# First-layer products of chunk pairs by Strassen's identity, in an S4D plus Mish kernel

## The chip, the core and the metric

The kernel runs on one core of one Trainium2 chip. The metric is the device time of one execution in microseconds (us); it is given as the median of three runs, and one more execution was recorded by the hardware profiler. A core has a matrix engine (TensorE, PE in the profile; PEld is its weight load), a vector engine (VectorE, DVE), an engine for activation functions (ScalarE, ACT), a general one (GpSimd, POOL) and one that issues transfers (SyncE, SP). Each takes its own queue of instructions in order; semaphores make one wait for another. TensorE writes its sums into PSUM, 128 partitions of eight banks; one bank holds 512 float32 per partition.

## The reference

```python
def _B_ref(x, w1, b1, w2):
    h = jnp.einsum("bsd,df->bsf", x, w1) + b1
    sp = jnp.log1p(jnp.exp(-jnp.abs(h))) + jnp.where(h > 0, h, jnp.zeros_like(h))
    act = h * jnp.tanh(sp)
    return jnp.einsum("bsf,fd->bsd", act, w2)

x = A_u
xn = _layernorm(x, axis=-1)
return x + _A_ref(xn, ...) + _B_ref(xn, B_w1, B_b1, B_w2)
```

There are 2048 tokens of 640 features; the hidden layer has 1728. `_A_ref` is a state-space convolution (S4D) of the normalised input. For the inputs given its kernel is so nearly a polynomial that the program does it with running sums over the tokens; a flag tells the cases in which that would not hold, and a general program stands behind the flag. The feed-forward part `_B_ref` holds nearly all of the arithmetic.

## The kernel before

The tokens are cut into four blocks b of 512, the hidden layer into 14 chunks f of 128 (chunk 8 has 64). A tile holds features on the partitions and a block's tokens along the columns. Float32 operands are split into two float16 numbers, high and low (`W1H`, `W1L`, `XH`, `XL`), and a product is three matmuls: high by high, low by high, high by low. The 640 features are five tiles of 128, so the first layer of a chunk (`mm1`) is 15 matmuls of 512 columns, and so is the second layer (`mm2`), which adds into five accumulators `ACC`, one bank each.

`step(b, f)` is one chunk: `mm1` of f into a first-layer accumulator, then the activation, then `mm2` of chunk f - 3 (`LAG`). The activation (Mish) alternates between ScalarE and VectorE: a sigmoid (`mish_0`, L611), `(h + bias) * s` on VectorE (`mish_v1`, L615), arctangent, square, hyperbolic tangent on ScalarE (L619, L623, L627), a product on VectorE (L631), the high half on ScalarE (L637) and the low half on VectorE (L647). The second part of chunk f - 1 is issued between the steps of chunk f.

The order is written by hand: `place` fills lists for each (b, f) that `step` issues at fixed points: `LOADS` (transfers from SP's queue), `V_` and `W_` (VectorE mostly), `A_` and `E_` (ScalarE), `PEX` (TensorE). They hold the side work: splitting weights and tokens into halves (`hi_w1`, `lo_w1`, `hi_w2`, `lo_w2`, `hi_x`, `lo_x`), the statistics and normalising of the next block (`stats`, `rstds`, `spread`, `norm_t`), the running sums (`skip_a` to `skip_d`, placed by the list `CONV`), taking the finished sums out of `ACC` (`join`), and sums of squares that check the weights' size (`chk`).

First-layer accumulators: two tiles `H[0]` and `H[1]` and a third, `TR`, a bank each. `bank` alternates between the two:

```python
H = [ps.tile([P, TB], F32, name=f"h{j}") for j in range(2)]
TR = ps.tile([P, TB], F32, name="tr")
return (H[0], H[1], TR)[f] if b == 0 and f < 3 else H[(f + 1) % 2]
```

## Time and profile before

| | |
|---|---|
| timed runs | 372.11, 372.90, 372.93 us; median 372.9 |
| profiled execution | 372.37 us, of it the profile's span 370.2 |
| block 0 / 1 / 2 / 3 of the span | to about 110, 200, 290, then the end |
| TensorE's granted clock | 0.998 of full speed |

A row of the timeline reads: start, time, engine, line, operation, what it writes from what, its size and count; in brackets the idle time of the engine before it and what ended it. The time of a matmul's row reaches to its modelled end and overlaps the next row's, so its pace is read from the starts. A row of a group (line, engine, operation) ends with busy time, mean time of one in ns and the idle time before. A row of the stretches has the length, then each engine's busy time with its count, then the granted clock, the transfers' share and GB/s.

### The profile page before, as it was taken

The numbers are of one execution on the slowest core, as the hardware profiler recorded it, in microseconds if no ns is written. First come the engines' busy times: TensorE is split into PE (matmuls) and PEld (weight loads), VectorE is DVE, ScalarE is ACT, GpSimd is POOL, SyncE is SP. The second block draws the span as 40 slices with busy tenths as digits, with TensorE's granted clock in tenths as the row PEclk, the third lists the DMA queues.
The fourth block names the chain that finished last, engine by engine and source line by source line (L and its number), as shares of the span: only waits on it lengthen the run. The fifth ranks groups of instructions, "written<-read, shape, count | busy, mean of one in ns | idle before, by whom it ended". The sixth has DMA issues, their size and how long they took to land.

```text
span 370.2 us, 4877 instructions
## 1 busy us (share of the span) xinstructions
PE 361.0 (98%) x1729; PEld 168.5 (46%) x1729; DVE 268.4 (72%) x455; ACT 271.5 (73%) x527; POOL 50.9 (14%) x72
## 2 busy tenths in 40 slices
PE   7999999999999999999999999999999999999992
PEld 6754444444444444444444444444444444444441
DVE  5969868995784987667547998666744787888632
ACT  3599896995767877776859787778767786887620
POOL 2100100000022051000013125100002332211000
PEclk9999999999999999999999999999999999999999
DMA  7867942900009747313256974712100943323104
GB/s 232 298 200 233 353 146 78 337 12 0 3 5 185 230 138 179 97 38 104 67 142 142 229 191 127 185 63 63 32 0 6 159 118 90 79 34 58 28 2 148
DMA packets 24302, 44.74 MB, mean 121 GB/s; under 512 B 3384, under 2 KB 6736, under 8 KB 24272
## 3 DMA queue, kind: packets, MB, share of 16 engines
q1 hardware_dynamic: 17424, 30.28, 25.6%
q0 software_dynamic: 6240, 13.11, 17.9%
q10 hardware_dynamic: 608, 0.98, 0.8%
q8 instruction: 15, 0.25, 0.3%
q14 instruction: 15, 0.12, 0.1%
HBM read 35.17 MB, written 5.26 MB: 109 GB/s over the span
## 4 chain that ended last, share of the span: by engine, by line
PE 95%; DMA 2%; issue 0%; ACTq 0%; ACT 0%; DVE 0%
PE h L559 45%; PE acc L586 14%; PE acc L587 14%; PE acc L588 14%; DMA w1s<-in_w_dram 2%; PE h L538 1%; PE acc L581 1%; PE acc L570 1%; PE acc L583 1%; PE acc L580 1%; PE tr L538 1%; PE acc L574 1%; PE acc L821 0%; PE acc L599 0%; PE acc L596 0%
## 5 line engine op out<-in xcount | busy, mean ns | idle before, releaser
L559 PE MATMUL h<-xh,w1h 128*128 128x512 f16 x265 | 92.0, 379 | 0.0
L588 PE MATMUL acc<-hi,w2l 128*128 128x512 f16 x235 | 89.1, 379 | 0.0
L587 PE MATMUL acc<-lo,w2h 128*128 128x512 f16 x235 | 89.1, 379 | 0.0
L586 PE MATMUL acc<-hi,w2h 128*128 128x512 f16 x235 | 89.1, 379 | 0.0
L559 PE MATMUL h<-xh,w1l 128*128 128x512 f16 x245 | 86.3, 379 | 0.0
L559 PEld LDWEIGHTS <-w1h 128*128 128x128 f16 (+1 forms) x534 | 50.5, 98 | 63.7 <-issue 4.6
L615 DVE SCALAR_TENSOR_TENSOR A<-h,bs,s 128x512 f32<-128x512 f32 x51 | 38.1, 747 | 57.0 <-ACT s L611 56.9
L611 ACT ACTIVATE s<-h,cv 128x512 f32<-128x512 f32 x51 | 34.9, 684 | 60.0 <-PE h L559 58.8
L559 PE MATMUL h<-xl,w1h 128*128 128x512 f16 (+2 forms) x269 | 63.8, 377 | 0.0
L647 DVE SCALAR_TENSOR_TENSOR lo<-A,hi 128x512 f16<-128x512 f32 x52 | 35.9, 690 | 16.6 <-ACT hi L637 16.6
L623 ACT ACTIVATE p<-p,kc 128x512 f32<-128x512 f32 (+1 forms) x56 | 40.4, 722 | 1.7
L619 ACT ACTIVATE p<-s,kc 128x512 f32<-128x512 f32 (+1 forms) x56 | 39.8, 711 | 0.1
L627 ACT ACTIVATE s<-p,kc 128x512 f32<-128x512 f32 (+1 forms) x56 | 39.8, 711 | 0.0
L631 DVE SCALAR_TENSOR_TENSOR A<-s,A 128x512 f32<-128x512 f32 (+1 forms) x56 | 38.1, 681 | 1.6 <-ACT s L627 1.5
L559 PEld LDWEIGHTS <-w1l 128*128 128x128 f16 x245 | 24.0, 98 | 28.5
L637 ACT ACTIVATE hi<-A 128x512 f16<-128x512 f32 (+1 forms) x56 | 34.4, 614 | 2.1 <-DVE A L631 2.1
L586 PEld LDWEIGHTS <-w2h 128*128 128x128 f16 x235 | 23.1, 98 | 27.6
L588 PEld LDWEIGHTS <-w2l 128*128 128x128 f16 x235 | 23.0, 98 | 27.7
L587 PEld LDWEIGHTS <-w2h 128*128 128x128 f16 x235 | 23.0, 98 | 27.3
L368 POOL DMA_DIRECT2D res<-in_xT_dram x15 | 13.5, 992 | 123.8 <-DVE res L661 113.1
L508 DVE TENSOR_TENSOR_SCAN g<-g,car,kc 128x512 f32<-128x512 f32 x20 | 25.6, 1279 | 0.0
L512 DVE TENSOR_TENSOR_SCAN g<-g,car,g 128x512 f32<-128x512 f32 x20 | 25.3, 1265 | 0.0
(142 smaller groups left out, 367.9 us busy)
## 6 DMA issues: line engine op xcount, KB each, us to landing
chk<-in_w2T_dram SPq DMA_DIRECT2D x15, 288.0 KB, 3.6
w2s<-in_B_w_dram SPq DMA_DIRECT2D x13, 320.0 KB, 3.9
chk<-in_w1T_dram SPq DMA_DIRECT2D x13, 320.0 KB, 4.1
xrow<-in_A_u_dram SPq DMA_DIRECT2D x12, 320.0 KB, 4.3
xt<-in_xT_dram SPq DMA_DIRECT2D x15, 256.0 KB, 7.4
res<-in_xT_dram POOLq DMA_DIRECT2D x15, 256.0 KB, 5.7
xt<-res POOLq DMA_DIRECT2D x15, 256.0 KB, 3.3
out_dram<-xt POOLq DMA_DIRECT2D x15, 256.0 KB, 2.7
```

What stands on the lines that cost most here:

```text
L559: pe.matmul(o, w, x, start=(j == 0), stop=(j == len(order) - 1))
L586: pe.matmul(ACC[k], W2H[f][:, c[k]], hi, start=False, stop=False)
L587: pe.matmul(ACC[k], W2H[f][:, c[k]], lo, start=False, stop=False)
L588: pe.matmul(ACC[k], W2L[f][:, c[k]], hi, start=False, stop=en)
L611: a.activation(s, h, AF.Sigmoid, bias=cv[:n, f:f + 1], scale=1 / SH)
L615: v.scalar_tensor_tensor(A, h, bs[:n, f:f + 1], s, op0=OP.add, op1=OP.mult)
L619: a.activation(p, s, AF.Arctan, bias=one[:n], scale=-1.0)
L623: a.activation(p, p, AF.Square, bias=pi4[:n], scale=2.0)
L627: a.activation(s, p, AF.Tanh, bias=mb[:n], scale=MG)
L631: v.scalar_tensor_tensor(A, s, MC, A, op0=OP.add, op1=OP.mult)
L637: a.activation(hi[:n], A, AF.Copy, scale=MA * SA / SH)
L647: v.scalar_tensor_tensor(lo, A, MA * SA / SH, hi[:n], op0=OP.mult, op1=OP.subtract)
```

## The change

In blocks 1 to 3 the first layer of two neighbouring chunks (0 and 1, 2 and 3, 4 and 5, 6 and 7, 9 and 10, 11 and 12) is computed together. Two chunks by two halves of the tokens by two pairs of feature tiles make a 2 x 2 by 2 x 2 block product, which Strassen's identity (in the form with fifteen additions) does with seven products instead of eight; a product here is two feature tiles, each in three matmuls of 256 columns. The fifth feature tile is added in the plain way, with one of its four products through a difference. That is 54 matmuls of 256 columns per pair instead of 30 of 512. Chunks 8 and 13 and block 0 stay as they were.

The operands need sums: of weights (`load_s`, `sum_w`, `hi_s`, `lo_s`: once per pair, in block 0 and early in block 1, from weights loaded again) and of tokens (`sum_x`, `hi_t`, `lo_t`: once per block). Partial results are shared: the first product `PV` is copied to SBUF, `PX` is copied to `PY` by ScalarE, and VectorE adds `PY` and `PV` into `PZ` and later into `PW`, onto which TensorE adds the remaining products. The three first-layer accumulators become slices of one PSUM tile `HT` of three banks. `pair(b, f)` is the new unit: the products come in four groups, with matmuls of the second layer between them. The side work moves in the lists (`place`, `CONV`), the list `E_` goes, and buffers are regrouped (`stt` 3 to 2, the checks share the weights' buffers and square in place). The flag gets six more conditions (`RATIO`).

```diff
-    H = [ps.tile([P, TB], F32, name=f"h{j}") for j in range(2)]
-    TR = ps.tile([P, TB], F32, name="tr")
+    HT = ps.tile([P, 3 * TB], F32, name="h")
+    TR, *H = (HT[:, j * TB:(j + 1) * TB] for j in range(3))
+    PV, PX, PZ, _, PY, PW = (HT[:, j * (TB // 2):(j + 1) * (TB // 2)] for j in range(6))
+    PVS = tmp.tile([P, TB // 2], F32, name="pvs")
...
+    def sum_w(i):
+        (a11, a12), (a21, a22) = ([t[:, 0:4].rearrange("p (q j) f -> p q j f", j=2)[:, :, j] for j in range(2)]
+                                  for t in SW.pop(i))
...
+        v.tensor_tensor(s1, a21, a22, op=OP.add)
+        v.tensor_tensor(s2, s1, a11, op=OP.subtract)
+        v.tensor_tensor(s3, a11, a21, op=OP.subtract)
+        v.tensor_tensor(s4, a12, s2, op=OP.subtract)
...
-        return (H[0], H[1], TR)[f] if b == 0 and f < 3 else H[(f + 1) % 2]
+        return (H[0], H[1], TR)[f] if b == 0 and f < 3 else H[(f + 1) % 2] if b == 0 else H[0]
...
+        return (lambda: (prod(PV, plain_w(1, 0), sums_x(1), True), prod(PX, plain_w(0, 0), plain_x(0, 0), True)),
+                lambda: (prod(PX, plain_w(0, 1), plain_x(1, 0)), prod(PX, last_w(0), last_x(0)),
+                         prod(PY, sums_w(2), sums_x(2))),
+                lambda: (prod(PY, sums_w(3), sums_x(3)), prod(PY, last_w(1), last_x(1)),
+                         prod(PZ, sums_w(4), plain_x(1, 1)), prod(PZ, last_w(0), last_x(1))),
+                lambda: (prod(PY, plain_w(1, 1), sums_x(4)), prod(PY, last_w(1), [(EH, EL)])))
...
         h = bank(b, f)[:n]
+        if b > 0 and n == P and f < LAST:
+            h = HT[:, TB // 2:3 * TB // 2] if f in PAIRS else H[1]
...
-                W_[b, i + 2].append(lambda b=b, i=i: stats(b + 1, i))
-            LOADS[b, 5].append(lambda b=b: load_xt(b + 1))
-            W_[b, 5].append(rstds)
-            PEX[b, 7] = spread
...
+                W_[b, i + 1].append(lambda b=b, i=i: stats(b + 1, i))
+            LOADS[b, 4].append(lambda b=b: load_xt(b + 1))
+            W_[b, 4].append(rstds)
+            PEX[b, 6] = spread
+            for k, f in enumerate((7, 8, 8, 9, 10)):
+                W_[b, f].append(lambda b=b, k=k: norm_t(b + 1, k, NX["bc"]))
+                A_[b, f + 1].insert(0, lambda b=b, k=k: hi_x(b + 1, k))
+                W_[b, f + 1].insert(0, lambda b=b, k=k: lo_x(b + 1, k))
+            for j, f, m in ((0, 10, 11), (1, 10, 11), (2, 11, 12), (3, 11, 13), (4, 11, 13)):
+                W_[b, f].append(lambda b=b, j=j: sum_x(b + 1, j))
+                A_[b, m].append(lambda j=j: hi_t(j))
+                W_[b, m].append(lambda j=j: lo_t(j))
+
+        for i, (t, at) in enumerate((((0, 5), (0, 7)), ((0, 8), (0, 10)), ((0, 11), (0, 12)),
+                                     ((1, 1), (1, 2)), ((1, 3), (1, 4)), ((1, 5), (1, 6)))):
+            LOADS[t].append(lambda i=i: load_s(i))
+            W_[at].append(lambda i=i: sum_w(i))
+            A_[at[0], at[1] + 1].append(lambda i=i: hi_s(i))
+            W_[at[0], at[1] + 1].append(lambda i=i: lo_s(i))
...
-    CONV = [((1, 4 + k), 0, k) for k in range(4)] + [((2, 0), 0, 4)] + [((2, 3 + k), 1, k) for k in range(KD)]
-    CONV += [((2, 13), 2, 0)] + [((3, 2 + k), 2, k) for k in range(1, KD)] + [((3, 7 + k), 3, k) for k in range(KD)]
+    CONV = [((1, 4), 0, 0), ((1, 6), 0, 1), ((1, 13), 0, 2), ((2, 0), 0, 3), ((2, 1), 0, 4)]
+    CONV += [((2, f), 1, k) for k, f in enumerate((2, 4, 5, 6, 7))]
+    CONV += [((2, 13), 2, 0)] + [((3, f), 2, k + 1) for k, f in enumerate((0, 1, 2, 4))]
+    CONV += [((3, f), 3, k) for k, f in enumerate((5, 6, 7, 8, 9))]
...
+    def pair(b, f):
+        one, two, three, four = mm1_pair(b, f)
+        A = mm2_ops((f - LAG) % NF)
+        p = PEND[0]
+        q = PEND[1] if len(PEND) > 1 else None
+        PEND[:] = [f, f + 1]
+        do(LOADS, (b, f))
+        one()
+        mish_a3(p)
+        mish_v3(p)
+        a.copy(PVS, PV)
+        a.copy(PY, PX)
+        if q is not None:
+            mish_a2(q)
+        run(A[:9])
+        mish_a4(p)
+        do(V_, (b, f))
+        mish_v4(p)
+        if q is not None:
+            mish_a3(q)
+            mish_v3(q)
+        two()
+        v.tensor_tensor(PZ, PY, PVS, op=OP.add)
...
+        if q is not None:
+            mish_a4(q)
+            mish_v4(q)
+        run(A[9:])
+        do(A_, (b, f))
+        do(W_, (b, f))
+        do(LOADS, (b, f + 1))
+        B = mm2_ops((f + 1 - LAG) % NF)
+        run(B[:3])
+        three()
+        v.tensor_tensor(PW, PY, PVS, op=OP.add)
...
+        do(V_, (b, f + 1))
+        do(A_, (b, f + 1))
+        mish_0(b, f)
+        mish_v1(f)
+        mish_a1(f)
+        mish_a2(f)
+        run(B[3:9])
+        four()
+        do(W_, (b, f + 1))
+        mish_0(b, f + 1)
+        mish_v1(f + 1)
+        mish_a1(f + 1)
+        run(B[9:])
...
-            step(b, f)
+            pair(b, f) if b > 0 and f in PAIRS else step(b, f)
```

The order of TensorE where the second layer gives way to the first, around chunk 5 of block 1. Before: `h0` is the accumulator, `w1h5` chunk 5's weights.

```order
L587 MATMUL acc4_195<-lo_1265,w2h1_141 128x512
L588 LDWEIGHTS w2l1_155
L588 MATMUL acc4_195<-hi_1257,w2l1_155 128x512
L559 LDWEIGHTS w1h5_118
L559 MATMUL h0_188<-xh10_173,w1h5_118 128x512 [waits DVE_49]
L559 LDWEIGHTS w1l5_132
L559 MATMUL h0_188<-xh10_173,w1l5_132 128x512
```

And now, at the beginning of the fourth group of the pair of chunks 4 and 5 (`h_210` is `HT`, `th3` a sum of tokens):

```order
L674 LDWEIGHTS w2l2_156
L674 MATMUL acc2_214<-hi_1537,w2l2_156 128x512
L642 LDWEIGHTS w1h5_118
L642 MATMUL h_210<-th3_203,w1h5_118 128x256 [waits DVE_49]
L642 LDWEIGHTS w1l5_132
```

This group waits for VectorE a second time within the pair. The beginning of the next pair, chunks 6 and 7:

```order
L674 MATMUL acc4_216<-lo_1540,w2h2_142 128x512
L674 LDWEIGHTS w2l2_156
L674 MATMUL acc4_216<-hi_1537,w2l2_156 128x512
L642 LDWEIGHTS w1h7_120
L642 MATMUL h_210<-th0_200,w1h7_120 128x256 [waits DVE_49]
```

Counted by the increments of VectorE's semaphore in the built program, the wait before was for `mish_v1` of chunk 3, two chunks back. Of the two waits now, the first is for `mish_v1` of chunk 4, of the same pair (L706 in the changed file), the second for `mish_v1` of chunk 5.

The order of VectorE at the same place. Before, between `lo` of chunk 3 and `mish_v1` of chunk 5 (L508 and L512 are the scans, which the listing names by their general form):

```order
L647 SCALAR_TENSOR_TENSOR lo<-A,hi 128x512 [waits PE_49,Activation_49]
L397 BN_STATS st<-xrow 128x6 [waits DMAHW2_49]
L398 BN_STATS st<-xrow 128x6
L399 BN_AGGR mv<-st 128x2 [waits DVE_49]
L512 SCALAR_TENSOR_TENSOR g_1320<-g_1320,car,g_1319 128x512
L514 SCALAR_TENSOR_TENSOR xt<-xt,cc,g_1320 128x512 [waits DVE_49]
L615 SCALAR_TENSOR_TENSOR A<-h_188,bs,s 128x512 [waits Activation_49]
```

Now, from `lo` of chunk 3 to `mish_v1` of chunk 4 (`ss` are weight sums, `g` the running sum, `pvs` the copy of `PV`):

```order
L738 SCALAR_TENSOR_TENSOR lo<-A,hi 128x512 [waits Activation_49]
L458 BN_STATS st<-xrow 128x6 [waits DMAHW7_49]
L459 BN_STATS st<-xrow 128x6
L460 BN_AGGR mv<-st 128x2 [waits DVE_49]
L416 TENSOR_TENSOR ss<-ws 128x256 [waits DMAHW1_49]
L417 TENSOR_TENSOR ss<-ss,ws 128x256 [waits DMAHW0_49,DVE_49]
L418 TENSOR_TENSOR ss<-ws 128x256
L419 TENSOR_TENSOR ss<-ws,ss 128x256 [waits DVE_49]
L578 SCALAR_TENSOR_TENSOR g_1458<-g_1458,car,g_1457 128x512
L580 SCALAR_TENSOR_TENSOR xt<-xt,cc,g_1458 128x512 [waits DVE_49]
L944 TENSOR_TENSOR h<-h,pvs 128x256 [waits PE_49]
L706 SCALAR_TENSOR_TENSOR A<-h,bs,s 128x512 [waits Activation_49]
```

The four weight sums and the second partial sum (L944) are new in this row of work, and it now ends with the step for which TensorE's fourth group waits. ScalarE's row at this place, from the check of the weights to the sigmoid of chunk 4:

```order
L532 ACTIVATE chk,q_105<-chk 128x640 [waits DMAHW5_49]
L591 COPY car<-g_1457 128x1
L592 COPY car<-g_1458 128x1 [waits DVE_49]
L429 ACTIVATE w1h_123<-ss 128x2x128
L429 ACTIVATE swh_192<-ss 128x256
L429 ACTIVATE swh_192<-ss 128x512
L532 ACTIVATE chk,q_105<-chk 128x640 [waits DMAHW6_49]
L568 ACTIVATE g_1622<-xt,cc 128x512
L569 COPY g_1622<-car 128x1
L570 ACTIVATE g_1623<-xt,cc 128x512 [waits Activation_49]
L702 ACTIVATE s<-h,cv 128x512 [waits DVE_49]
```

Before, a sigmoid stood directly behind the `skip_a` steps and waited for TensorE alone; now the carry copy waits for the scan of the same pair, the weights' high halves stand between, and the sigmoid waits for VectorE's partial sum.

## The prediction

> **What bounds the kernel now.** I read the page's busy line and its chain that ended last first, then what the two vector engines wait for, then the stretches.

> ```profile
> PE 361.0 (98%) x1729; PEld 168.5 (46%) x1729; DVE 268.4 (72%) x455; ACT 271.5 (73%) x527; POOL 50.9 (14%) x72
> PE 95%; DMA 2%; issue 0%; ACTq 0%; ACT 0%; DVE 0%
> ACT s L611 <- PE h L559: 58.8, 37, 3.3
> DVE A L615 <- ACT s L611: 60.9, 43, 3.6
> 110.50:200.00 89.50, 89.50 (x421) 40.24 (x419) 60.16 (x89) 68.57 (x139) 15.56 (x20) 1.00 0.50 129
> 363.50:370.20 6.70, 0.03 (x1) 0.00 (x0) 0.77 (x3) 0.00 (x0) 0.00 (x0) 0.86 0.37 126
> ```

> TensorE is 95% of the chain and is busy through the whole of block 1 (110.5 to 200). The idle time lies elsewhere: ScalarE waits 58.8 us for the first layer to end, VectorE 60.9 us for ScalarE's sigmoid. So fewer columns through TensorE shorten the span, as long as nothing new makes TensorE wait. Since `bank` alternates between two tiles, it can run two chunks ahead of the activation.

> **What the change removes.** A pair of chunks had 30 first-layer matmuls of 512 columns and gets 54 of 256.

> ```profile
> 16.42 1.25 PE L538 MATMUL h<-xl,w1h 128*128 128x256 f16 x10
> 17.52 1.24 PE L538 MATMUL h<-xh,w1l 128*128 128x512 f16 x5
> L538 PEld LDWEIGHTS <-w1h 128*128 128x128 f16 x60 | 5.7, 98 | 1.9 <-ACT w1h L373 1.1
> 117.47 1.24 PE L559 MATMUL h<-xl,w1h 128*128 128x512 f16 x5
> 118.55 0.38 PE L586 MATMUL acc<-hi,w2h 128*128 128x512 f16 x1
> ```

> Ten matmuls of 256 take 17.52 - 16.42 = 1.10 us, 0.110 each, with ten weight loads of 98 ns among them; five of 512 take 118.55 - 117.47 = 1.08, 0.216 each. A pair's first layer goes from 30 x 0.216 = 6.48 to 54 x 0.110 = 5.94, and 18 pairs save 9.7 us. With its 30 second-layer matmuls a pair lasted 12.96 and would last 12.42.

> [...]

> **What the change adds: two waits in every pair.** The accumulators were tiles of their own and are now slices of one tile, and the built program orders all readers and writers of that tile. By its semaphore counts, in each of the 18 pairs the first matmul of the fourth group (`four`) waits for VectorE's first step on the even chunk (`mish_v1(f)`, L706 in the changed file), and the first matmul of the next pair waits for `mish_v1(f + 1)`. Neither touches the columns that these matmuls write. The sigmoid of the even chunk in turn waits for the second partial sum on VectorE. The durations:

> ```profile
> 118.75 0.69 ACT L611 ACTIVATE s<-h,cv 128x512 f32<-128x512 f32 x1 [1.26 <-PE h L559]
> 119.33 0.71 ACT L627 ACTIVATE s<-p,kc 128x512 f32<-128x512 f32 x1
> 119.94 0.71 ACT L619 ACTIVATE p<-s,kc 128x512 f32<-128x512 f32 x1
> 120.69 0.72 ACT L623 ACTIVATE p<-p,kc 128x512 f32<-128x512 f32 x1
> 121.32 0.61 ACT L637 ACTIVATE hi<-A 128x512 f16<-128x512 f32 x1
> 121.84 0.72 ACT L472 ACTIVATE sq<-chk 128x640 f32<-128x640 f32 x1
> 122.56 0.71 ACT L502 ACTIVATE g<-xt,cc 128x512 f32<-128x512 f32 x1
> 123.25 0.72 ACT L504 ACTIVATE g<-xt,cc 128x512 f32<-128x512 f32 x1
> 119.47 0.75 DVE L615 SCALAR_TENSOR_TENSOR A<-h,bs,s 128x512 f32<-128x512 f32 x1 [2.25 <-ACT s L611]
> 120.14 0.68 DVE L631 SCALAR_TENSOR_TENSOR A<-s,A 128x512 f32<-128x512 f32 x1
> 120.74 1.28 DVE L508 TENSOR_TENSOR_SCAN g<-g,car,kc 128x512 f32<-128x512 f32 x1
> 121.97 0.69 DVE L647 SCALAR_TENSOR_TENSOR lo<-A,hi 128x512 f16<-128x512 f32 x1
> 122.57 0.49 DVE L397 BATCH_NORM_STATS2 st<-xrow 128x6 f32<-128x320 f32 x1
> 123.61 1.23 DVE L512 TENSOR_TENSOR_SCAN g<-g,car,g 128x512 f32<-128x512 f32 x1
> 124.88 0.75 DVE L514 SCALAR_TENSOR_TENSOR xt<-xt,cc,g 128x512 f32<-128x512 f32 x1
> L827 DVE SCALAR_TENSOR_TENSOR xl<-acc,xh 128x256 f16<-128x256 f32 x10 | 3.7, 416 | 0.0
> 14.75 1.74 DVE L827 SCALAR_TENSOR_TENSOR xl<-acc,xh 128x256 f16<-128x256 f32 x5
> 8.11 1.49 ACT L824 ACTIVATE xh<-acc 128x256 f16<-128x256 f32 x5 [0.23 <-PE acc L821]
> ```

> From these: 0.20 from the end of a stream on TensorE to its reader (118.55 to 118.75); sigmoid to VectorE's step 0.72 (118.75 to 119.47), that step 0.75; in a row, 0.60 for a step over 512 columns, 1.27 for a scan, 1.04 for the statistics (122.57 to 123.61). No row shows the new 256-column sums: bounds are 0.35 (five in 1.74) and, doubled for a sum whose result stays in PSUM, 0.83. I take 0.42, the duration of one alone, since the nearest row reads PSUM too. An ACT copy of 256 is 0.30 (five in 1.49).

> Clock of a pair without waits, from its first matmul: `one` ends at 12 x 0.110 = 1.32; nine of the second layer to 3.26; `two` (15) to 4.91; nine to 6.85; `three` (18) to 8.83; six to 10.13; `four` (9) to 11.12; six to 12.42.

> *A pair with empty lists.* After `three`: 0.20 + 0.42 + 0.72 + 0.75 = 2.09 until `four` may start; six second-layer matmuls cover 1.30, so TensorE waits 0.79. After `four`: 0.20 + 0.72 + 0.75 = 1.67, cover 1.30, wait 0.37. That is 1.16 per pair and 20.9 over 18, twice the saving. The first partial sum (4.91 + 0.20 + 0.42 = 5.53, due 6.85) and ScalarE's copies (1.32 + 0.20 + 0.60 = 2.12, due 3.26) are covered; without cover each would cost its 0.6 to 0.8.

> *A pair with lists.* VectorE's and ScalarE's side work (statistics, weight sums, scans, normalising) stands in their queues ahead of the very steps that TensorE now waits for. Chunks 4 and 5 of block 1: VectorE ends the first partial sum at 5.53, `lo` at 6.14, statistics 7.18, four weight sums 8.6, scan 9.85, the combining step 10.6, the second partial sum 11.0. ScalarE reaches its carry copies near 6.0 and waits for that scan to 9.85, then 1.1 for the new weights' high halves (two of 256, one of 512), 0.72 check (121.84 to 122.56), 1.4 for the two `skip_a` steps: the sigmoid starts at 13.1, `mish_v1` ends at 14.55 against a due time of 10.13. `four` ends at 15.54, and 1.67 later, at 17.2, the next pair starts: 4.8 late. The same walk with the lists that `place` gives the others, in us beyond 12.42: block 1: 3.5, 4.0, 4.8, 4.2, 3.5, 3.1; block 2 (scans of block 1 and statistics, no weight sums): 3.8, 3.5, 2.4, 3.3, 3.5, 3.1; block 3 (scans only): 2.8, 2.3, 2.0, 1.9, 1.2, 1.2. Sum 54.1. At the entry to blocks 2 and 3 ScalarE's list of chunk 13 (new high halves, check, `skip_a`) makes the copies 1.0 late: 2.0. Together 56.1, of which 20.9 are the bare chain.

> **Block 0** keeps its matmuls, but its three accumulators lie in the same tile, so chunk f waits for `mish_v1(f - 1)` instead of f - 2.

> ```profile
> 20.77 1.24 PE L559 MATMUL h<-xh,w1h 128*128 128x512 f16 x5
> 25.55 0.75 DVE L615 SCALAR_TENSOR_TENSOR A<-tr,bs,s 128x512 f32<-128x512 f32 x1 [0.90 <-ACT s L611]
> 64.50 0.68 DVE L420 TENSOR_TENSOR xt<-xt,bc 128x512 f32<-128x512 f32 x1
> 65.21 0.69 DVE L421 TENSOR_TENSOR xt<-xt,bc 128x512 f32<-128x512 f32 x1
> 65.82 0.74 DVE L615 SCALAR_TENSOR_TENSOR A<-h,bs,s 128x512 f32<-128x512 f32 x1
> 67.08 0.81 DVE L383 SCALAR_TENSOR_TENSOR w2l<-w2s,w2h 128x640 f16<-128x640 f32 x1
> 67.81 0.81 DVE L377 SCALAR_TENSOR_TENSOR w1l<-w1s,w1h 128x640 f16<-128x640 f32 x1
> L439 DVE TENSOR_REDUCE mx<-par 128x10 f32<-128x1280 f32 x1 | 1.5, 1479 | 0.0
> L443 DVE SCALAR_TENSOR_TENSOR junk<-par,dt 128x128 f32<-128x128 f32 x10 | 2.9, 348 | 0.0
> 363.52 0.75 DVE L652 SCALAR_TENSOR_TENSOR xt<-h,xt 128x256 f32<-128x256 f32 x2
> ```

> Chunk 3 starts at 20.77 now and must wait for chunk 2's step, which ends at 25.55 + 0.75 = 26.30: 5.5. From chunk 7 on VectorE's list per chunk passes the 6.48 of TensorE. Chunk 7's: three steps of a chunk 1.9, two weight remainders 1.5, some ten tiny steps 1.5, the reduction 1.5, four products 1.7, the normalising that is moved there 1.3, the new weight sums 1.4: 10.8. The lists of 8, 10 and 11 come to 8.1, 8.3 and 7.4. I make that 4.8, 2.3, 1.5 and 0.9 of TensorE time, 15.0 with the start. At the end the last half's matmuls wait for the drain of the first half, which is in the same tile: 0.4 (two take 0.75).

> The added weight and token loads (SP's queue) feed sums a chunk or more later; POOL's accumulating DMAs keep their order. I cost both at nothing: the transfers lie under 60 to 70 us of vector work per block, and uncovered one would cost its landing of some 4 us once.

> **Sum** against the profiled execution's own 372.4: -9.7 + 56.1 + 15.0 + 0.4 gives 434.2; the median of the timed runs is 0.5 above it, so **434 us** is forecast.

> **Rivals.**
> *The lists are ahead of time*, and only the bare chain is left: 372.4 - 9.7 + 20.9 + 5.5 + 0.4 = 389.5. For it: VectorE and ScalarE idle over a quarter of the span. Against: they are in-order queues, and the lists stand ahead of the awaited step in the program.
> *The end on the other side: the activation chain fits under the second layer.* Place: after `three`. If the reader chain of 2.09 were under the 1.30 of cover, TensorE would never wait and the saving would stay: 372.4 - 9.7 = 362.7, up to 371 with a few list waits. It decides at 0.79 us per pair, and each of the four links has its row, so I see little for it.
> *The clock falls in the gaps.* The last stretch shows a granted clock of 0.86 with TensorE idle, 1.00 where it is busy. If the gaps of 3 to 5 us (the start of block 0, chunk 7, the pairs of block 1) each bring a stretch at a lower clock, some eight of them at 1 to 2 us make 442 to 450.
> [...]
> *The extra weight loads show*: 18 x 24 x 0.098 = 42 us on top, 476, which the ten matmuls in 1.10 us speak against.

> **How the numbers follow.** Forecast 0.66, its own range 415 to 446 (the chains' terms together 15% off either way); lists ahead of time 0.12; clock 0.17; the chain fits 0.03; weight loads 0.01; 0.01 for others. The range that holds 8 in 10 is 408 to 452. A change under 0.3% (1.1 us) can't be told from none. Faster takes the 0.03, less the chance that list waits eat it: 0.02; the same 0.01; slower 0.97.

> **What would show it.** TensorE's idle time in the profile after should be some 70 us, put down to VectorE's `mish_v1` line at two places in each pair, first-layer matmuls still 0.110 apart; the stretch of block 1 should be the longest (some 20 us more than before), block 3 the shortest; chunk 3 of block 0 should start near 26. It is wrong if TensorE waits mainly for the copies, the partial sums or DMAs, or if block 0 keeps its length.

## The result, and the profile after

The changed kernel takes 453.6 us (median of 4, 451.0 to 456.5) against 372.8 for the kernel before on the same chip: a ratio of 1.217, 95% interval 1.210 to 1.225. The forecast was 434 us with a range of 408 to 452: the sign is right, and the time lies 1.6 us above the range. The profiled execution took 453.4 us, 451.6 of it span.

Three rows of the page of the changed kernel: the busy line, TensorE's granted clock in 40 slices, and the chain that ended last by engine.

```profile
PE 372.3 (82%) x2161; PEld 214.1 (47%) x2161; DVE 317.0 (70%) x567; ACT 304.1 (67%) x596; POOL 49.9 (11%) x72
PEclk9969997999998969999699999999999999999998
PE 39%; DVE 33%; ACT 22%; issue 3%; DMA 2%; POOL 0%; SPq 0%; ACTq 0%; DVEq 0%
```

TensorE was 95% of the chain and is 39%; VectorE (33%) and ScalarE (22%) are most of the rest. TensorE's busy time rose from 361.0 to 372.3 us although it streams fewer columns, and four of the 40 slices show a granted clock of 0.6 or 0.7: part of its work ran slower.

What TensorE waited for (in us: total, times, longest):

```profile
PE h L642 <- DVE A L706: 42.1, 28, 4.4
PE h L622 <- DVE A L706: 15.6, 8, 9.2
PE h L642 <- ACT h L920: 5.8, 6, 1.7
PE h L622 <- DVE A L699: 4.6, 1, 4.6
```

L642 is a pair's first layer, L622 an ordinary chunk's, L706 is `mish_v1`, L699 the sum by which VectorE reads chunk 8's two halves, L920 the copy of `PX` to `PY`. The idle time put down to `mish_v1` is what the forecast named.

The stretches of the two kernels, block by block (start and end, length, busy time of PE, PEld, DVE, ACT and POOL, granted clock, DMA share, GB/s). A block's stretch begins here with the first matmul of its first layer; the ends at about 110, 200 and 290 us given for the kernel before lie some three chunks later, where a block's last second-layer sums are done. First the kernel before, then the changed one, the last stretch with the tail:

```profile
0.00:89.41 89.41, 86.93 (x445) 45.25 (x445) 73.97 (x157) 71.51 (x123) 5.16 (x16) 1.00 0.60 196
89.41:177.48 88.07, 88.07 (x414) 39.54 (x412) 63.35 (x114) 65.20 (x132) 13.14 (x16) 1.00 0.41 103
177.48:265.55 88.07, 88.07 (x414) 39.51 (x412) 62.38 (x91) 69.26 (x144) 16.60 (x20) 1.00 0.51 130
265.55:370.20 104.65, 97.98 (x462) 44.24 (x460) 68.67 (x96) 65.52 (x134) 15.96 (x20) 0.99 0.30 64
```

```profile
0.00:112.71 112.71, 91.95 (x444) 45.92 (x445) 85.92 (x183) 76.17 (x132) 5.17 (x16) 0.92 0.48 152
112.71:229.05 116.34, 95.27 (x557) 56.57 (x556) 78.02 (x154) 76.54 (x153) 9.95 (x12) 0.91 0.38 114
229.05:336.23 107.18, 87.47 (x558) 53.44 (x557) 78.82 (x119) 79.54 (x167) 18.80 (x24) 1.00 0.42 109
336.23:451.60 115.37, 97.58 (x606) 58.20 (x604) 74.21 (x113) 71.89 (x147) 16.02 (x20) 0.99 0.27 58
```

Block by block that is:

| stretch | forecast | measured | of it at half pace |
|---|---|---|---|
| block 0 | +15.0 | +23.3 | 5.2 |
| block 1 | +19.9 | +28.3 | 8.5 |
| block 2 | +17.4 | +19.1 | 0 |
| block 3 and tail | +9.6 | +10.7 | 0 |

The forecast's column is its lists per block plus 1.0 at the entries to blocks 2 and 3 and 0.4 at the end, less a third of the 9.7 in blocks 1 to 3. Block 1 grows most and block 3 least, as foretold; blocks 2 and 3 come out within 1.7 us. Both misses lie where the clock column drops, to 0.92 and 0.91.

The fourth group of pair 4|5 in block 1, from the timeline of TensorE (start, duration, and in brackets the idle time before it):

```profile
155.20 0.38 PE L674 MATMUL acc<-hi,w2l 128*128 128x512 f16 x1
159.93 0.37 PE L642 MATMUL h<-th,w1h 128*128 128x256 f16 x1 [4.35 <-DVE A L706]
160.09 0.42 PE L642 MATMUL h<-th,w1l 128*128 128x256 f16 x1
160.31 0.42 PE L642 MATMUL h<-tl,w1h 128*128 128x256 f16 x1
...
164.79 0.42 PE L642 MATMUL h<-tl,w1h 128*128 128x256 f16 x1
165.00 0.33 PE L642 MATMUL h<-th,w1h 128*128 128x256 f16 x1
165.17 0.27 PE L642 MATMUL h<-th,w1l 128*128 128x256 f16 x1
165.28 0.27 PE L642 MATMUL h<-tl,w1h 128*128 128x256 f16 x1
```

After the wait the matmuls start 0.21 us apart, which is half pace; from 165.17 on it is 0.11 again. Read in this way (each start against the one before, less 0.109 for 256 columns or 0.216 for 512), six stretches ran at half pace and lost 2.8, 2.4, 1.5, 2.5, 1.8 and 2.7 us: 13.7 in all, behind idle times of 9.2, 4.6, 2.5, 4.4, 2.5 and 3.4. TensorE's idle rows add up to 73.6 us, against 2.4 in the kernel before. To each wait belong another 0.16 us, by which a matmul's shown 0.38 exceeds its 0.216; that makes some 80 us of gaps.

### The profile page after: what moved, and what is told of

Read it like the earlier page. It is cut to its first block, busy times and chain, and to the rows that moved or that the text cites. A ratio compares the mean times of both kernels' runs of the same rounds, so it can differ in the third digit from the quotient of the medians.

```text
span 451.6 us, 5979 instructions
## 1 busy us (share of the span) xinstructions
PE 372.3 (82%) x2161; PEld 214.1 (47%) x2161; DVE 317.0 (70%) x567; ACT 304.1 (67%) x596; POOL 49.9 (11%) x72
## 3 DMA queue, kind: packets, MB, share of 16 engines
q0 software_dynamic: 6240, 13.11, 14.1%
## 4 chain that ended last, share of the span: by engine, by line
PE 39%; DVE 33%; ACT 22%; issue 3%; DMA 2%; POOL 0%; SPq 0%; ACTq 0%; DVEq 0%
PE h L642 16%; PE acc L674 13%; PE h L622 7%; DVE A L706 6%; ACT s L702 4%; DVE g L578 2%; DVE lo L738 2%; DVE xt L482 2%; PE h L604 2%; DVE xl L400 2%; DVE xt L481 2%; ACT p L718 2%; DVE A L722 2%; ACT hi L728 2%; DVE g L574 2%
## 5 line engine op out<-in xcount | busy, mean ns | idle before, releaser
L674 PE MATMUL acc<-hi,w2h 128*128 128x512 f16 x275 | 103.2, 385 | 0.0
L706 DVE SCALAR_TENSOR_TENSOR A<-h,bs,s 128x512 f32<-128x512 f32 x52 | 38.7, 745 | 53.4 <-ACT s L702 53.4
L642 PE MATMUL h<-th,w1h 128*128 128x256 f16 x72 | 20.6, 286 | 42.1 <-DVE A L706 42.1
L642 PEld LDWEIGHTS <-w1l 128*128 128x128 f16 x216 | 21.5, 100 | 61.9 <-issue 57.8
L642 PEld LDWEIGHTS <-w1h 128*128 128x128 f16 x432 | 43.3, 100 | 12.8 <-issue 1.5
L722 DVE SCALAR_TENSOR_TENSOR A<-p,A 128x512 f32<-128x512 f32 (+1 forms) x56 | 38.4, 685 | 8.9 <-ACT p L718 8.9
L622 PE MATMUL h<-xh,w1h 128*128 128x512 f16 x85 | 26.2, 412 | 20.2 <-DVE A L706 15.6
L714 ACT ACTIVATE p<-p,kc 128x512 f32<-128x512 f32 (+1 forms) x56 | 40.3, 720 | 1.2
L718 ACT ACTIVATE p<-p,kc 128x512 f32<-128x512 f32 (+1 forms) x56 | 39.6, 708 | 0.0
L642 PE MATMUL h<-xh,w1h 128*128 128x256 f16 x126 | 34.3, 273 | 5.8 <-ACT h L920 5.8
L622 PEld LDWEIGHTS <-w1h 128*128 128x128 f16 (+1 forms) x174 | 16.3, 105 | 44.0 <-issue 29.9
L642 PE MATMUL h<-xl,w1h 128*128 128x256 f16 x126 | 34.3, 272 | 0.0
L642 PE MATMUL h<-xh,w1l 128*128 128x256 f16 x126 | 34.3, 272 | 0.0
```

Of the source, the lines that this page charges most:

```text
L622: pe.matmul(o, w, x, start=(j == 0), stop=(j == len(order) - 1))
L642: pe.matmul(o, p, q, start=start and n == 1, stop=n == 3 * len(w), skip_group_check=True)
L674: pe.matmul(o, w, x, start=start, stop=stop)
L706: v.scalar_tensor_tensor(A, h, bs[:n, f:f + 1], s, op0=OP.add, op1=OP.mult)
L714: a.activation(p, p, AF.Square, bias=pi4[:n], scale=2.0)
L718: a.activation(p, p, AF.Tanh, bias=mb[:n], scale=MG)
```

## The experiments

Four theories stood: (A) TensorE waits because everything that touches the one tile `HT` is ordered; (B) the pairs' own copies, partial sums and side work hold it up whatever the tiles; (C) the half pace follows from the idle time; (D) it has another cause. Later ones arose from the results.

**Separate tiles.** In `e1_three_tiles` the three banks are three tiles, and the even chunk's activation is split where `PX` and `PZ` meet:

```diff
-    HT = ps.tile([P, 3 * TB], F32, name="h")
-    TR, *H = (HT[:, j * TB:(j + 1) * TB] for j in range(3))
-    PV, PX, PZ, _, PY, PW = (HT[:, j * (TB // 2):(j + 1) * (TB // 2)] for j in range(6))
+    TR, *H = (ps.tile([P, TB], F32, name=c) for c in ("tr", "h0", "h1"))
+    PV, PX, PZ, _, PY, PW = (t[:, c] for t in (TR, *H) for c in (CA, CB))
...
+        parts = [(CA, PX), (CB, PZ)] if b > 0 and f in PAIRS else [(slice(0, TB), h)]
...
+        for c, h in parts:
+            a.activation(s[:, c], h, AF.Sigmoid, bias=cv[:n, f:f + 1], scale=1 / SH)
```

> The changed kernel with its three accumulator banks as three tiles again (the same columns of PSUM), and the sigmoid and VectorE's first step of an even chunk in two halves of 256 columns, since they now lie in two tiles. Theory A (TensorE waits because all that reads or writes the shared tile is ordered): the first matmul of the fourth group no longer waits for mish_v1 of the even chunk, nor the next pair for mish_v1 of the odd one, and block 0 goes back to waiting for the chunk two before; the 78 us of gaps fall to under 15 and the stretches at half pace vanish, 363 to 375 us. Rival B (the seven products' own partial sums and copies, and the side work ahead of them in the queues, hold TensorE up whatever the tiles): the gaps move to the copies (L920) and the partial sums and the time stays over 400 us.

`e2_two_tiles` keeps `PX` and `PZ` in one tile of two banks:

```diff
+    HT, H1 = (ps.tile([P, n * TB], F32, name=f"h{n}") for n in (2, 1))
+    TR, *H = HT[:, 0:TB], HT[:, TB:2 * TB], H1
...
-        return (H[0], H[1], TR)[f] if b == 0 and f < 3 else H[(f + 1) % 2] if b == 0 else H[0]
+        return (H[1], TR, H[0])[f] if b == 0 and f < 3 else H[f % 2] if b == 0 else H[0]
```

> The changed kernel with two tiles: one of two banks that holds PV, PX, PZ, so that the even chunk's sigmoid stays one instruction of 512 columns, and one of one bank with PY and PW; in block 0 chunks 0, 1, 2 take H1, TR, H0 and the chunks after them H1 and H0 in turn. Theory A: what counts is that PY and PW (written by the fourth group) are apart from PX and PZ (read by the even chunk's activation): as with three tiles, 363 to 375 us, within 3 us of it. Rival B: over 400 us.

They took 403.7 us (ratio to before 1.084, 1.082 to 1.085) and 408.6 us (1.095, 1.093 to 1.098). TensorE's waits with three tiles:

```profile
PE tr L641 <- ACT h L922: 20.5, 8, 6.4
PE h L641 <- DVE h L946: 4.9, 6, 1.7
PE h L621 <- DVE A L708: 3.9, 5, 1.4
```

Theory A is right in what it names: 49.9 of the 80.8 us go with the shared tile, the waits for `mish_v1` shrink from 57.7 us to under 5, and block 0 loses its start wait. It is wrong in what it leaves: 403.7, not 363 to 375. TensorE now waits for the copy (L922 here) and the second partial sum (L946), which stand in their engines' queues; the longer wait had, as it seems, hidden most of that (5.8 us at the copy in the changed kernel). Rival B is right about the remaining 31 us. Two tiles cost 4.8 us more, where the small chunk 8 and the transposes share a tile with a pair's products: TensorE waits 3.7 us for chunk 8's sum (L699) and 2.3 for a transpose's turn.

**The shared tile alone.** `e3_before_one_tile` is the kernel before with its accumulators in one tile:

```diff
-    H = [ps.tile([P, TB], F32, name=f"h{j}") for j in range(2)]
-    TR = ps.tile([P, TB], F32, name="tr")
+    HT = ps.tile([P, 3 * TB], F32, name="h")
+    TR, *H = (HT[:, j * TB:(j + 1) * TB] for j in range(3))
```

> The kernel before, with nothing changed but its three first-layer accumulators made slices of one tile; no seven products. Theory A: chunk 3 of block 0 waits for chunk 2's first VectorE step, 5.5 to 9.2 us, with a stretch at half pace of some 2.5 us behind it; from there on a chunk's first-layer matmuls wait for the step of the chunk just before, 1.67 us after its matmuls end, which the second layer's 3.24 us cover except where side work stands ahead: 382 to 396 us. Rival B (the shared tile costs nothing by itself): 372 to 375 us.

387.1 us (1.039, 1.038 to 1.041), inside theory A's range. Its waits for the tile:

```profile
PE h L559 <- DVE A L615: 9.2, 1, 9.2
PE h L559 <- DVE A L608: 1.9, 1, 1.9
```

With ordinary chunks the one tile costs 14.3 us, 11 of it at the start (9.2 of waiting, 1.6 at half pace, 0.2 of a matmul's end); in blocks 1 to 3 the second layer covers a chunk's chain as worked out. So the tile alone costs 14.3, the pairs with separate tiles 31.0, and both together 80.8: 35.5 us come only of the two together, where a pair's chain is ordered through the tile.

**The half pace.** `e4_keep_busy` fills the waits with 201 matmuls of 0.216 us whose weights are zero, before chunks 3, 9, 12 and 13 of block 0 and before the fourth group of 16 pairs:

```diff
+    def keep(b, n, start=False):
+        for _ in range(n):
+            pe.matmul(ACC[0], zw, XH[b % 2][0], start=start, stop=start)
...
         run(B[3:9])
+        keep(b, KEEP.get((b, f), 0))
         four()
```

> The changed kernel with extra matmuls in the places where TensorE waited most (before chunks 3, 9, 12, 13 of block 0, and before the fourth group of 16 pairs): their weights are zero, they add 0 to an accumulator of the second layer, and there are a few less than the wait had room for. The waits stay as they are. Theory C (the half-pace stretches come from TensorE being idle): the 14 us that matmuls ran over their full pace go, the granted clock is near 1.00, and the time falls to 438 to 446 us. Rival D (matmuls are slow after a wait for another reason, such as the vector engines' work at that time): the stretches at twice the spacing stay, 451 to 458 us.

447.4 us, granted clock 0.994. The clock row of its page, and TensorE's two largest waits:

```profile
PEclk9999999899999999999999999999999999999999
```

```profile
PE h L644 <- DVE A L708: 16.1, 29, 1.6
PE h L624 <- DVE A L708: 7.2, 8, 2.8
```

All stretches at half pace are gone but one, which lost 1.4 us behind a wait of 2.8 us that was left in block 0. So theory C holds and D falls. But the time falls by 6.3 us and not by 13: TensorE reaches its next wait earlier, and the vector engines' lists are not done sooner. The idle rows that are left (34.9 us) and the 43.4 us of filling make 78.3 us where 73.6 stood. The expected 438 to 446 us were missed by 1.4 for that reason.

**The order of the queues.** `e8_step_first` keeps the one tile and puts the odd chunk's lists behind the even chunk's step:

```diff
-        do(V_, (b, f + 1))
-        do(A_, (b, f + 1))
         mish_0(b, f)
         mish_v1(f)
+        do(V_, (b, f + 1))
+        do(A_, (b, f + 1))
         mish_a1(f)
```

> The changed kernel, one tile, with the odd chunk's two lists (V_ and A_) put behind the even chunk's sigmoid and first VectorE step instead of ahead of them. Theory A3 (a list costs TensorE time because it stands ahead of the awaited step): the 35 us of waits before the fourth groups fall towards their 0.73 us each, and the time to 425 to 440 us. Rival F (the same work then stands ahead of the odd chunk's sigmoid, and the wait before the next pair grows by as much): 450 to 465 us, with the waits before the next pair's first matmul several times their 7 us.

The runs took 456.0 to 463.1 us, with a ratio to before of 1.232 (1.225 to 1.239) where the changed kernel has 1.217: not faster. Summed over the rows of its timeline, the waits before the fourth groups fall from 34.1 to 20.2 us, and those before the next matmul of the first layer rise from 10.4 to 30.0: rival F. The lists have to run in any place; where both chunks of a pair are awaited, there is no place for them ahead of either.

`e5_lists_after_copies` (three tiles) moves the lists of chunks 8 and 13 behind the copies of the pair that follows:

```diff
-        do(A_, (b, f))
-        do(W_, (b, f))
+        if (b, f + 1) > (0, LAST) and not end and f in (HALF, LAST):
+            LATE.append((b, f))
+        else:
+            do(A_, (b, f))
+            do(W_, (b, f))
...
         a.copy(PY, PX)
+        do_late()
```

> Three tiles as before, and one move of the order: where a single chunk (8 or 13) stands ahead of a pair, its lists of side work for ScalarE and VectorE come behind the pair's two copies (L922 there) and not ahead of them. With three tiles the six entries 0|13 to 1|0, 1|8 to 1|9, 1|13 to 2|0 and so on waited 6.4, 3.9, 1.5, 4.6, 1.4 and 2.1 us for the copies. Theory A2 (what is left of the loss is side work ahead of a step that TensorE waits for, and its place in the queue decides): the lists are 2.6 us long before block 1 and 1 to 2 elsewhere, so some 8 us of those 20 go and 3 to 4 us at half pace with them: 390 to 397 us. Rival F (the vector queues have no room left there, and the work only moves into the next wait): 400 to 405 us.

401.1 us. The waits for the copy fall from 20.5 to 12.5 us, as theory A2 had it, and the waits for the first partial sum rise from nothing to 6.8, as rival F had it. TensorE's idle rows add up to 34.4 us before and 34.3 after. The 2.6 us gained are half pace: behind the waits it falls from 5.7 to 1.3 us, and the transposes at the start of this profiled execution take 1.6 us more. F is right.

**Fewer pairs.** If a queue with room is what a pair needs, pairs should pay in block 3, whose VectorE and ScalarE have least to do. `e6_block3` has three tiles and pairs in block 3 alone (`PB` is 3); `e7_no_pairs` is its control without any (`PB` is 4); `e9_block3_b` mends what `e6_block3` showed late.

```diff
-            pair(b, f) if b > 0 and f in PAIRS else step(b, f)
+            pair(b, f) if b >= PB and f in PAIRS else step(b, f)
```

> Three tiles, pairs by seven products in block 3 alone; blocks 1 and 2 by ordinary chunks, the weight sums moved to blocks 2 and 3, the scans of blocks 0 to 2 to blocks 1 and 2, the lists behind the copies at the entries, and a few steps of a pair in another order. Theory A2: six pairs save 6 x 0.54 = 3.2 us, and where the queues have room TensorE hardly waits (with three tiles block 3 had one wait of 2.1 us, at its chunk 8): 368 to 371 us, below the kernel before. Rival G (a pair costs more than it saves wherever it stands): 373 us or more.

> The kernel e6_block3 with no pairs in any block and no weight sums, all else the same: the control for it. Theory A2: the gain of e6_block3 is that of the seven products, so this one is 2 to 4 us slower than it and within 1.5 us of the kernel before, 371 to 374 us. Rival H (the gain is that of the side work's new places): as fast as e6_block3.

375.6 us (1.008, 1.007 to 1.010) against 372.5 for the control (0.999, 0.998 to 1.000): six pairs cost 3 us on balance. The timelines of VectorE, ScalarE and TensorE in `e6_block3`, up to the second group of pair 4|5:

```profile
295.96 0.42 DVE L416 TENSOR_TENSOR ss<-ws 128x256 f32<-128x256 f32 x1 [2.84 <-DMA ws<-in_w_dram]
297.43 0.75 DVE L709 SCALAR_TENSOR_TENSOR A<-h,bs,s 128x512 f32<-128x512 f32 x1
298.21 0.36 ACT L932 COPY h<-tr 128x256 f32<-128x256 f32 x1 [3.18 <-DVE A L709]
298.62 0.27 PE L642 MATMUL tr<-xh,w1h 128*128 128x256 f16 x1 [1.41 <-ACT h L932]
```

A load of weights that lands late holds a weight sum; behind it stands chunk 3's step, behind that the copy of pair 4|5, behind that TensorE.

> e6_block3 again with what its trace showed late moved: its pairs saved 3.2 us of matmuls against e7_no_pairs and lost 5.7 to waits, 2.0 at the entry of block 3 (the copies behind the check and chunk 13's steps), 1.4 where the weight sums of pair 9 had waited 2.8 for their load, 1.3 for the second partial sum of that pair, 0.6 at chunk 8 and 0.4 in the start. Here the weight loads come two to four chunks before their sums, the sums of four pairs lie in chunks 4 to 9 of block 2, the checks begin two chunks earlier, the fourth group follows the second partial sum at once and VectorE's step of the even chunk comes behind it. Theory A2 (where no side work stands ahead of an awaited step the saving shows): 369 to 371.5 us, faster than the kernel before. Rival G (some wait always remains that eats the 3.2 us): 372.5 to 375 us.

375.7 us, and the wait had moved again: block 3 lost only 2.5 us to waits, but the normalising and the weight sums that now share block 2 delayed two ordinary chunks there by 2.8 us, with 1.7 us of half pace behind them. That is rival G's reading a second time, 0.7 us above its range.

`e10_three_pairs` (three tiles) takes the last three pairs of block 3 only, with the scans of block 3 ahead of them and the weight sums between them; within a pair no matmuls of the second layer stand between the third and the fourth group now. `e11_control` is the same without the pairs.

```diff
+USE = (6, 9, 11)
...
-            pair(b, f) if b > 0 and f in PAIRS else step(b, f)
+            pair(b, f) if b >= PB and f in USE else step(b, f)
```

> Only the last three pairs of block 3 (chunks 6|7, 9|10, 11|12) by seven products; the scans of block 3 in its chunks 0 to 4 and the weight sums in chunks 4, 6 and 8 of it, so that no entry of a block and no crowded chunk of block 2 is touched, and every load comes at least one chunk ahead. Three pairs save 3 x 0.54 = 1.6 us. Theory A2 (a pair gains where neither VectorE nor ScalarE has side work ahead of an awaited step): TensorE has no wait over 0.5 us in block 3 and the time is 370.5 to 372 us, 1 to 2 us below its control. Rival G (some wait always eats the saving): 372.5 to 374.5 us.

> The kernel e10_three_pairs with ordinary chunks all through and no weight sums, all else the same: its control. Both theories: 372 to 373.5 us, as the kernel before; theory A2 has it 1 to 2 us above e10_three_pairs, rival G at or below it.

371.2 us, ratio to before 0.9957 (0.9943 to 0.9971); the control 372.6 (0.9997, 0.9988 to 1.0006). All the waits of TensorE in `e10_three_pairs` lie in its first 13 us:

```profile
PE acc L1000 <- DVE x L984: 1.8, 3, 0.9
PE tr L1014 <- POOL car L333: 1.5, 1, 1.5
PE h L605 <- DVE w1l L389: 0.2, 1, 0.2
```

Three pairs were to save 1.6 us and save 1.4 against the control. This is the one version here that takes less time than the kernel before, by 0.4%.

## Why the prediction was right or wrong

**What a pair saves: right, and a little low.** In pair 4|5 the fourth group was due 10.13 us after the pair's start; the six matmuls ahead of it end their stream at 155.42, 10.10 after 145.32. First-layer matmuls are 0.11 apart at full pace; at 0.109 by the starts, against 0.110 in the forecast, the 18 pairs save 10.7 us and not 9.7.

**The waits in the pairs: right in place, near in size.** 56.1 us were forecast. Measured are 44.5 us of idle time before fourth groups and first matmuls, 5.8 at the copies (2.0 forecast), 1.8 at the transposes and the flag (not forecast), and 41 matmul ends of 0.16 (not forecast either): 58.7. The sums of 256 columns into PSUM take 0.43 us each (L931 and L944, 18 times each) for 0.42 forecast; the upper bound of 0.83 was the author's estimate, and no row shows a doubling. The walk through pair 4|5 came out to the tenth. Rows of ScalarE's and VectorE's timelines of the changed kernel:

```profile
157.11 0.71 ACT L568 ACTIVATE g<-xt,cc 128x512 f32<-128x512 f32 x1
157.80 0.72 ACT L570 ACTIVATE g<-xt,cc 128x512 f32<-128x512 f32 x1
158.43 0.67 ACT L702 ACTIVATE s<-h,cv 128x512 f32<-128x512 f32 x1
159.13 0.75 DVE L706 SCALAR_TENSOR_TENSOR A<-h,bs,s 128x512 f32<-128x512 f32 x1 [2.88 <-ACT s L702]
```

The sigmoid starts 13.11 us after the pair (13.1 forecast) and the step ends at 14.56 (14.55). The bare chain shows in the last pair, whose lists are empty: 0.73 and 0.27 us of idle time and twice 0.16, against 0.79 and 0.37.

**The start of block 0: wrong in size, 9.2 for 5.5.** The step took chunk 2's `mish_v1` at the time the profile before shows for it. But that step is late itself:

```profile
20.58 0.69 ACT L702 ACTIVATE s<-h,cv 128x512 f32<-128x512 f32 x1 [4.86 <-PE h L604]
29.01 0.70 DVE L706 SCALAR_TENSOR_TENSOR A<-h,bs,s 128x512 f32<-128x512 f32 x1
29.76 2.29 PE L622 MATMUL h<-xh,w1h 128*128 128x512 f16 x5 [9.22 <-DVE A L706]
```

The matmuls of chunks 0, 1 and 2 are all issued ahead of the first sigmoid, which reads the same tile, so it waits for the last of them. In the kernel before it starts 3.41 us earlier, which is the most of the missing 3.7:

```profile
17.17 0.69 ACT L611 ACTIVATE s<-h,cv 128x512 f32<-128x512 f32 x1 [1.07 <-PE h L538]
```

`e3_before_one_tile` shows the same 9.2 with no pairs. The lists further on in block 0 came out near in size and not in place: 9.5 us were forecast, and TensorE's waits are 4.6, 0.4, 2.4 and 1.2 us, before chunks 9, 10, 12 and 13. The forecast's four lists, less 6.48 each, add up to 8.7, and it does not say how 9.5 came of them; as the places differ too, the near agreement is partly luck.

By the waits above, the tile of three banks is ordered as a whole and takes 453.6 us; three tiles of one bank, each ordered by itself, take 403.7. The order across the banks costs 49.9 us here.

**The clock: the step that failed.** The forecast summed its own gaps of 3 to 5 us and then let every matmul after them run at full pace; the clock stood apart as a rival at 0.17, "some eight of them at 1 to 2 us make 442 to 450". The 1 to 2 us, and that gaps of 3 to 5 us bring a lower clock, were the author's estimate: no row of the kernel before shows either ahead of its last stretch, and measured are 1.5 to 2.8 us behind six waits of 2.5 to 9.2. The clock was no alternative but a consequence of the forecast, which so put it at nothing in its sum: waits of 5.5, 4.8 and 4.4 us stood in the forecast itself (the start, chunk 7, pair 4|5), and the last section shows that waits of that length bring half pace. Six stretches lost 13.7 us, and `e4_keep_busy` shows that idleness is their cause. 434.2 + 13.7 + 3.7 at the start gives 451.6 for the profiled execution's 453.4; the waits in the pairs (2.6 more) less the saving (1.0 more) are most of the rest. The forecast's own range was also drawn loosely: 15% of the 71.1 us of waits is 10.7, which gives 423 to 445 and not 415 to 446.

**The other rivals.** Lists ahead of time (389.5) and a chain that fits (362.7) fell with the table of waits. Weight loads do not show: the matmuls of 256 columns keep their 0.11, with loads of 0.10 us (L642) among them. Costing the added loads at nothing was right for this kernel; with pairs in block 3 one of them cost 2.8 us of VectorE's time.

## What to carry to other kernels

Where TensorE was busy for 98% of the span, a change that made it wait cost twice: of the eight waits of 2.5 us and more here, six lost another 1.5 to 2.8 us to half pace behind them. Such a term belongs in the sum and not in a case beside it. But what filling the waits won back was less than that (6.3 us of 13.7), since the awaited engines were no faster. Before giving up tiles for slices of one, list who reads and writes each slice and take the order of the whole tile as issued, from its first reader on. An identity that trades matmul columns for steps on in-order engines paid here only where those engines had nothing else in front of the awaited steps: 18 pairs lost 81 us, three that were placed so won 1.4.

## What the runs showed of the hardware

Not every gap of the same length brings half pace. In the changed kernel the granted clock falls to 0.50 at 25.16, 72.95, 141.22, 158.28, 178.76 and 216.31 us, and all the times between these are whole multiples of 3.41 us (14, 20, 5, 6 and 11 of them). Stretches of the changed kernel cut at such steps, in the columns above:

```profile
137.80:141.22 3.42, 1.29 (x6) 0.49 (x5) 1.49 (x3) 3.39 (x8) 0.88 (x1) 1.00 0.89 190
141.22:144.63 3.41, 3.08 (x12) 1.77 (x12) 2.75 (x8) 1.90 (x4) 0.00 (x0) 0.50 1.08 287
212.90:216.31 3.41, 1.34 (x7) 0.49 (x5) 1.79 (x4) 2.80 (x7) 0.00 (x0) 1.00 0.00 0
216.31:219.72 3.41, 2.13 (x10) 1.47 (x10) 1.35 (x2) 1.90 (x4) 0.00 (x0) 0.50 0.01 2
322.12:325.54 3.42, 1.63 (x10) 0.74 (x8) 2.09 (x5) 2.52 (x6) 0.00 (x0) 1.00 0.00 0
325.54:328.95 3.41, 1.91 (x14) 1.33 (x14) 1.35 (x3) 2.81 (x6) 0.00 (x0) 1.00 0.00 0
328.95:332.36 3.41, 3.14 (x16) 1.32 (x15) 2.10 (x3) 2.57 (x4) 0.00 (x0) 1.00 0.00 0
```

They hold waits of 2.46, 3.35 and 3.29 us. The first leaves TensorE idle for 62% of one stretch (1.29 us busy of 3.42), the second for 61%, and in each case the next stretch runs at 0.50. The third is cut in two by a step, which leaves 52% and 44%, and the clock stays at 1.00. The DMA share of the stretch at 0.50 is 1.08 behind the first wait and 0.01 behind the second, so that transfers do not tell them apart.
